# A recurrence and a gated MLP in one kernel: low weight parts and word shifts on VectorE, with a new order of the first part

## The chip, the cores and the metric

The kernel runs on one core of a Trainium2 chip. The metric is the device time of one execution in microseconds. Before the change the median of three runs is 610.35 us (609.67 to 611.15).

## The reference, cut to what matters

A recurrence over 768 tokens (4 batches, 8 heads of 48 channels) gives `y`; its heads, put side by side, are the 3072 x 384 input `x` of a gated MLP with 1536 hidden columns.

```python
for t in range(S):
    cur = einsum('bhd,bhe->bhde', u * k[t], v[t])
    y[t] = einsum('bhd,bhde->bhe', r[t], state + cur)
    state = w * state + einsum('bhd,bhe->bhde', k[t], v[t])
...
gate = 1.0 / (1.0 + np.exp(-(x @ w_gate)))
val = x @ w_val
return gate * val @ w_out
```

All inputs and the output are float32.

## The kernel before, in words

**The recurrence** is computed in chunks of 64 tokens. There are 12 chunks and each is done in two groups of heads, so there are 24 groups, numbered n = 0 to 23. One group takes these steps, each with a letter that the order uses:

- `L.n`, `X.n`: SyncE issues the loads of the chunk by channel (`chan`, three buffers) and by token (`toks`, three buffers).
- `A.n` (ScalarE), `R.n` (`queries`, L265, GpSimd), `k.n` (`keys`, L271, VectorE), `T.n` (`token_keys`, L275, GpSimd): queries and keys times powers of the decay. `A` and `R` write `dec` (two buffers).
- `Z.n` (`scores`): 64 small matmuls into one PSUM tile of two banks, which has one buffer. `K.n` (`keep`, L322, VectorE) copies the masked entries into one of two `score` tiles.
- `I.n` (`apply`) and `O.n` (`outer`): small matmuls into two PSUM banks; with them comes the reading of the old state (`from_state`). `I` gives the chunk's result, `O` what the state gains.
- `h.n` (ScalarE) and `l.n` (`x_low`, L406, VectorE): the result is split into a rounded part and the rest, both written to `xt`, the input of the MLP. `d.n` (ScalarE) and `s.n` (`add_state`, L376, VectorE) decay the state and add to it. `F.n` (`fills`, L417) moves rows of `xt` by DMA on SyncE.

**The MLP** works on tiles of 512 tokens (two chunks), so a tile of tokens needs four groups. Its hidden columns come in 12 weight tiles f of 128. An item i is one token tile with one weight tile. The first token tile takes weight tile 0 in two halves of 256 tokens (items 0 and 1), then weight tiles 1 to 11 whole (items 2 to 12, so item i uses weight tile i - 1). The five other token tiles have 12 items each. One item is

- `U.i` (`up`, L436): 18 matmuls, 9 into each of two PSUM banks (every product is done as three passes over rounded parts and rests),
- `g.i` sigmoid of the first bank (ScalarE, L451), `m.i` product with the second (VectorE, L456), `H.i` the rounded part (ScalarE), `q.i` the rest (`h_low`, L465, GpSimd),
- `D.i` (`down`, L475): 9 matmuls into three accumulator banks.

The banks of `U.i` and of `I.n` come from one ring of three. So the matmuls of a step wait until the readers of the banks three allocations back are through: a sigmoid, a product, or a group's `h`, `l` and `s`.

**The weights** stay in memory once they are prepared, so only the first token tile pays for that. They come as the 64-bit words of double numbers, viewed as pairs of 32-bit words. For weight tile f:

- `W.f` (`load_weights`, L208): the load, 1152 words of 64 bits on each of 128 partitions.
- `c.f` (`scale_words`, L213, ScalarE): the upper word as a float times a power of two, into `wf` (two buffers).
- `j.f` (`join_words`, L219, VectorE): three integer operations on `wf`, on L224, L225 and L226: a shift by 3, the sign, and three bits of the lower word.
- `w.f` (`round_weights`, L228, ScalarE): the rounded part, `whi`. `o.f` (`rest_of_weights`, L234, GpSimd): the rest, `wlo`. Their tile lies in the buffer that the raw words came in.

Weight tile 0 is prepared in halves (`c0`, `j0`, `w0`, `o0`). `w` and `o` work in two halves for all weight tiles.

**The order.** Every engine works through its own instructions in program order, without a scheduler (L86). For the first part, up to item 12, that order is a text, `START` (L41); a loop at L543 calls one step after the other by the table at L525. An engine's own order is `START` with the steps of the others left out. Behind `START` a loop does the other 60 items with the 16 other groups in fixed slots; there `q`, `R` and `T` are on GpSimd.

A branch at the end for unusual decays is not taken with these inputs.

Of the kernel before, what the change touches and what calls it, by code (L numbers as in the profile page):

```python
# [37 lines left out]
HALF, FIRST = 1, 8  # L38
SLOTS = (0, 3, 6, 9)

START = """  # L41
tk tc L.0 L.1 ti.1 X.0 ti.0 A.0 tp X.1 R.0 A.1 W.0 R.1 k.0 tt k.1 tn Z.0 T.0 L.2 T.1 K.0 X.2
c0.0 I.0 c0.1 L.3 j0.0 A.2 R.2 Z.1 h.0 T.2 k.2 w0.0 l.0 O.0 A.3 R.3 K.1 F.0 X.3 o0.0 s.0 Z.2 W.1
j0.1 T.3 I.1 K.2 w0.1 O.1 W.2 h.1 o0.1 k.3 l.1 Z.3 c.1 s.1 F.1 L.4 j.1 I.2 X.4 c.2 W.3 O.2 h.2
R.4 d.2 l.2 T.4 K.3 w.1 F.2 W.4 A.4 o.1 s.2 j.2 I.3 W.5 h.3 O.3 d.3 l.3 w.2 s.3 F.3 L.5 k.4 U.0
c.3 o.2 X.5 j.3 W.6 A.5 Z.4 R.5 g.0 c.4 U.1 T.5 L.6 m.0 w.3 K.4 H.0 o.3 X.6 j.4 g.1 W.7 I.4 O.4
h.4 q.0 d.4 R.6 D.0 m.1 W.8 l.4 H.1 T.6 w.4 s.4 F.4 q.1 k.5 c.5 U.2 o.4 A.6 W.9 j.5 c.6 Z.5 W.10
g.2 D.1 j.6 w.5 U.3 o.5 L.7 m.2 w.6 X.7 K.5 H.2 W.11 o.6 g.3 k.6 c.7 I.5 m.3 H.3 j.7 Z.6 h.5 q.2
d.5 O.5 q.3 D.2 c.8 R.7 A.7 l.5 T.7 s.5 F.5 w.7 K.6 U.4 o.7 j.8 c.9 D.3 g.4 j.9 w.8 I.6 o.8 O.6
h.6 d.6 m.4 w.9 l.6 s.6 F.6 H.4 o.9 c.10 k.7 U.5 j.10 q.4 c.11 Z.7 g.5 m.5 D.4 w.10 K.7 H.5 o.10  # L50
j.11 U.6 q.5 w.11 D.5 g.6 o.11 m.6 I.7 H.6 O.7 h.7 d.7 q.6 l.7 F.7 s.7 U.7 D.6 g.7 m.7 H.7 U.8
q.7 D.7 g.8 m.8 H.8 U.9 q.8 D.8 g.9 m.9 H.9 L.8 X.8 U.10 q.9 D.9 g.10 m.10 H.10 U.11 q.10 D.10
g.11 m.11 H.11 U.12 q.11 A.8 R.8 k.8 T.8 D.11 g.12 m.12 H.12 q.12 D.12
"""


# [1 line left out]
def rwkv_then_moe(ctx: ExitStack, tc: tile.TileContext, wd, ch, tk, wt, rk0, vn0, wd0, out):  # L58
    nc = tc.nc

    const = ctx.enter_context(tc.tile_pool(name="const", bufs=1))
# [31 lines left out]
    w = wu[:, 0]  # L93
# [18 lines left out]
    score = [const.tile([P, 512], F32, name=f"score{i}") for i in range(2)]  # L112

    state = const.tile([P, 4 * N2 * D // 2 + 16], F32, name="state")
    zero = const.tile([P, 1], I32, name="zero")
    table = const.tile([P, 1], F32, name="table")

    def constants():
        make_identity(nc, ident)
        nc.gpsimd.memset(causal, 0.0)  # L120
        nc.gpsimd.affine_select(
            out=causal, in_=causal, compare_op=ALU.is_ge, fill=1.0, base=0,
            pattern=[[-1, P]], channel_multiplier=1,
        )
        for lo in (0, 64):
            nc.gpsimd.tensor_copy(masks[lo : lo + 64, 0], causal[lo : lo + 64, lo : lo + 64])
            nc.gpsimd.tensor_copy(masks[lo : lo + 64, 1], ident[lo : lo + 64, lo : lo + 64])
        nc.gpsimd.memset(zero, 0)
        for t in score:
            nc.gpsimd.memset(t, 0.0)  # L130
        nc.gpsimd.memset(state, 0.0)
        nc.scalar.activation(table, ident[:, 0:1], AF.Sigmoid)
# [7 lines left out]
    tabn = const.tile([P, N2, D], F32, name="tabn")  # L140
# [62 lines left out]

    W3, WH = 3 * DM, 3 * DM // 2
    raw, w32, wparts, whi, wlo = {}, {}, {}, {}, {}
    WHOLE, HALVES = (slice(0, W3),), (slice(0, WH), slice(WH, W3))

    def load_weights(f):  # L208
        raw[f] = wp.tile([P, W3], I64, name="wr", tag=f"w{f or NF - 1}")
        for c in HALVES if f == 0 else WHOLE:  # L210
            nc.sync.dma_start(out=raw[f][:, c], in_=wt[f, :, c])

    def scale_words(f, c):  # L213
        if f not in w32:
            w32[f] = wtmp.tile([P, W3], F32, name="wf")
        words = raw[f].bitcast(F32).rearrange("q (n two) -> q n two", two=2)
        nc.scalar.activation(w32[f][:, c], words[:, c, 1], AF.Copy, scale=2.0**-112)

    def join_words(f, c):  # L219
        words = raw[f].bitcast(I32).rearrange("q (n two) -> q n two", two=2)  # L220
        low, high = words[:, c, 0], words[:, c, 1]
        g = w32[f].bitcast(I32)[:, c]
        none = zero.broadcast_to([P, c.stop - c.start])
        nc.vector.scalar_tensor_tensor(g, g, 3, none, ALU.logical_shift_left, ALU.bitwise_or)  # L224
        nc.vector.scalar_tensor_tensor(g, high, -(2**31), g, ALU.bitwise_and, ALU.bitwise_or)  # L225
        nc.vector.scalar_tensor_tensor(g, low, 29, g, ALU.logical_shift_right, ALU.bitwise_or)  # L226

    def round_weights(f, c):  # L228
        if f not in wparts:
            wparts[f] = wp.tile([P, 2, W3], F32R, name="wx", tag=f"w{f}")  # L230
            whi[f], wlo[f] = wparts[f][:, 0], wparts[f][:, 1]
        nc.scalar.copy(out=whi[f][:, c], in_=w32[f][:, c])  # L232

    def rest_of_weights(f, c):  # L234
        nc.gpsimd.tensor_tensor(wlo[f][:, c], w32[f][:, c], whi[f][:, c], ALU.subtract)  # L235


    xt, dec, ga, yb = {}, {}, {}, {}
# [3 lines left out]
    def bc2(ap):  # L242
        n, m, k = ap.shape
        return ap.unsqueeze(2).broadcast_to([n, m, 2, k])

    def v4(ap):
        return ap.rearrange("q (m t i) -> q m t i", m=4, t=2)

    def dec_of(n):
        if n not in dec:  # L250
            dec[n] = adk.tile([P, 2, 512], F32, name="dec")
        return dec[n]

    def table_of(n):
        return tabk[:, 4 * GROUPS[n][1] : 4 * GROUPS[n][1] + 4]
# [6 lines left out]
                t[:, 1, cs], k[:, cs], AF.Copy, scale=wu[:, 1, 4 * g + m : 4 * g + m + 1]  # L262
            )

    def queries(n):  # L265
        t = dec_of(n)
        nc.gpsimd.tensor_tensor(  # L267
            v4(t[:, 0]), v4(chan[n][:, 0]), bc2(table_of(n)[:, :, ::-1]), ALU.mult
        )

# [1 line left out]
        k = chan[n][:, 1]  # L272
        nc.vector.tensor_tensor(v4(k), v4(k), bc2(table_of(n)), ALU.mult)

    def token_keys(n):  # L275
        k, g = toks[n][:, 0, 0 : 8 * D], GROUPS[n][1]
        nc.gpsimd.tensor_tensor(v4(k), v4(k), bc2(tabn[:, 4 * g : 4 * g + 4]), ALU.mult)  # L277

# [150 lines left out]
    class Moe:  # L431
# [30 lines left out]
            h = self.h[f] = hq.tile([P, 2, 512], F32R, name="h")  # L462
            nc.scalar.copy(out=h[:, 0, c], in_=sg[:, c])  # L463

        def h_low(self, f):  # L465
            c, h = self.cols, self.h[f]
            nc.gpsimd.tensor_tensor(h[:, 1, c], self.sg.pop(f)[:, c], h[:, 0, c], ALU.subtract)  # L467

        def gate(self, f):
            self.sigmoid(f)  # L470
# [18 lines left out]
    def accumulators():  # L489
        return [pacc.tile([P, 512], F32, name=f"acc{d}") for d in range(3)]  # L490
# [12 lines left out]
    items = [(0, h, f) for h, f in halves]  # L503
# [20 lines left out]

    steps = {  # L525
        "L": load_channels, "X": load_tokens, "W": load_weights, "A": bonus_keys, "R": queries,
        "k": keys, "T": token_keys, "Z": scores, "K": keep, "I": apply, "O": outer,
        "d": decay_state, "s": add_state, "h": x_high, "l": x_low, "F": fills, "D": finish,
        "tc": constants, "tk": channel_table, "ti": inverses, "tp": token_powers,
        "tt": token_turn, "tn": token_table,  # L530
        "c": lambda f: [scale_words(f, c) for c in WHOLE],
        "j": lambda f: [join_words(f, c) for c in WHOLE],
        "w": lambda f: [round_weights(f, c) for c in HALVES],
        "o": lambda f: [rest_of_weights(f, c) for c in HALVES],
        "c0": lambda j: scale_words(0, HALVES[j]), "j0": lambda j: join_words(0, HALVES[j]),
        "w0": lambda j: round_weights(0, HALVES[j]), "o0": lambda j: rest_of_weights(0, HALVES[j]),
        "U": lambda i: moe_of(items[i]).up(items[i][2]),
        "g": lambda i: moe_of(items[i]).sigmoid(items[i][2]),
        "m": lambda i: moe_of(items[i]).product(items[i][2]),
# [2 lines left out]
    }  # L542
    for step in START.split():  # L543
        name, _, arg = step.partition(".")
# [52 lines left out]
    with tc.If(bad != 0):  # L597
        with ExitStack() as g:
# [66 lines left out]
            with tc.For_i(0, NC, 2) as c:  # L665
# [11 lines left out]
                m = Moe(x, accumulators(), slice(0, 512))  # L677
# [93 lines left out]
```

## Time and profile before

| | us |
|---|---|
| median of three runs | 610.35 |
| the profiled execution, its own time | 604.38 |
| its span, first to last instruction | 602.4 |
| TensorE matmul busy in the span | 546.7 |
| VectorE busy | 215.6 |
| GpSimd busy | 205.0 |
| ScalarE busy | 191.0 |

In the profile PE is TensorE's matmuls, PEld its weight loads, DVE VectorE, ACT ScalarE, POOL GpSimd and SP SyncE. L with a number is a line of the kernel. A row of the groups gives line, engine, operation, output and inputs, shape and count, then busy time in us and the mean of one in ns, then the engine's idle time just before and what ended it. A row of a timeline gives start and duration in us, then the same names, and in brackets the idle time before it. A row of a stage gives the stretch and its length, then the busy time of each engine with the number of instructions, TensorE's granted clock, the DMA's share and GB/s.

### The profile page before, as it was taken

The page shows a single profiled execution, that of the slowest core. Times are in us where ns is not written, and L with a number is a line of the kernel's source. Part 1 is how long each engine was busy: PE and PEld are TensorE (multiplying, and loading weights), DVE is VectorE, ACT ScalarE, POOL GpSimd, SP SyncE. Part 2 cuts the span into 40 slices and gives each one's busy share as a digit, 9 for nine tenths or more (in the row PEclk, how much of TensorE's full clock was granted, in tenths as well). Part 3 has the DMA queues.
Part 4 walks back from the last instruction along what each step waited for, and adds up shares of the span by engine and source line. Part 5 has one row for each costly group of instructions (what it writes and reads, how often), then busy time and mean ns, then how long its engine had stood idle before and what let it go on. Part 6 is the DMA issues. An engine that isn't in the chain of part 4 may idle for free. (4 is left out here: it accounts for less than half of the span.)

```text
span 602.4 us, 12902 instructions
## 1 busy us (share of the span) xinstructions
PE 546.7 (91%) x5689; PEld 441.6 (73%) x5689; DVE 215.6 (36%) x317; ACT 191.0 (32%) x432; POOL 205.0 (34%) x159
## 2 busy tenths in 40 slices
PE   2747965989979999999999999999999999999994
PEld 2736754778768887878888878888878787888882
DVE  6799799921131232232133133133223112110101
ACT  4364464332232232242233143233233122222211
POOL 6448886732323233133133133133222311121120
PEclk9999768899999999999999999999999999999998
DMA  7479700020060020240020250020250001100001
GB/s 284 181 276 414 317 1 1 10 81 1 5 237 2 1 63 11 81 171 9 1 72 5 78 177 3 1 72 15 67 178 2 1 9 20 50 3 0 1 0 58
DMA packets 13117, 44.55 MB, mean 74 GB/s; under 512 B 2080, under 2 KB 2464, under 8 KB 11648
## 3 DMA queue, kind: packets, MB, share of 16 engines
q1 hardware_dynamic: 13056, 43.66, 20.9%
q8 instruction: 47, 0.77, 0.5%
q14 instruction: 14, 0.11, 0.1%
HBM read 36.58 MB, written 4.72 MB: 69 GB/s over the span
## 5 line engine op out<-in xcount | busy, mean ns | idle before, releaser
L445 PE MATMUL ring<-xt,wx 128*128 128x512 f32 (+1 forms) x1314 | 324.5, 401 | 8.1 <-DVE sg L458 5.6
L445 PEld LDWEIGHTS ring<-xt,wx 128*128 128x128 f32 x1314 | 249.2, 194 | 67.0 <-DVE sg L458 5.7
L467 POOL TENSOR_TENSOR h<-sg,h 128x512 fp32r<-128x512 f32 (+1 forms) x73 | 99.9, 1369 | 345.0 <-ACT h L463 345.0
L483 PE MATMUL acc<-h,wx 128*128 128x512 f32 (+1 forms) x657 | 164.9, 395 | 3.8 <-POOL h L467 3.4
L458 DVE TENSOR_TENSOR sg<-ring,sg 128x512 f32<-128x512 f32 (+1 forms) x73 | 49.9, 683 | 295.9 <-PE ring L445 293.2
L483 PEld LDWEIGHTS acc<-h,wx 128*128 128x128 f32 x657 | 121.7, 190 | 32.3 <-POOL h L467 4.5
L463 ACT CAST h<-sg 128x512 fp32r<-128x512 f32 (+1 forms) x73 | 44.8, 614 | 149.9 <-DVE sg L458 149.9
L454 ACT ACTIVATE sg<-ring 128x512 f32<-128x512 f32 (+1 forms) x73 | 43.2, 591 | 139.7 <-PE ring L445 139.6
L235 POOL TENSOR_TENSOR wx<-wf,wx 128x576 fp32r<-128x576 f32 x24 | 46.8, 1967 | 19.4 <-ACT wx L232 19.3
L325 DVE COPY_PREDICATED score<-masks,sc 128x512 f32<-128x512 int32 x48 | 36.0, 750 | 16.0 <-PE sc L317 15.2
L267 POOL TENSOR_TENSOR dec<-chan,tabk 128x512 f32<-128x512 f32 x24 | 33.6, 1402 | 12.4 <-DMA chan<-in_ch 10.0
L261 ACT ACTIVATE dec<-chan,wu 128x128 f32<-128x128 f32 x96 | 30.8, 401 | 7.7 <-DMA chan<-in_ch 7.3
L408 DVE TENSOR_TENSOR xt<-ring,xt 112x256 fp32r<-112x256 f32 (+1 forms) x52 | 19.9, 417 | 31.2 <-ACT xt L404 31.1
L286 PE MATMUL ring<-dec,state 48*48 48x64 f32 (+1 forms) x704 | 18.4, 235 | 13.7 <-DVE state L381 5.4
L286 PEld LDWEIGHTS ring<-dec,state 48*48 48x48 f32 (+1 forms) x704 | 14.6, 137 | 21.8 <-issue 12.2
L404 ACT CAST xt<-ring 112x256 fp32r<-112x256 f32 (+1 forms) x52 | 17.1, 374 | 41.1 <-PE ring L286 40.9
L225 DVE SCALAR_TENSOR_TENSOR wf<-wr,wf 128x1152 int32<-128x1152 int32 (+1 forms) x13 | 27.2, 2090 | 0.4
L277 POOL TENSOR_TENSOR toks<-toks,tabn 128x384 f32<-128x384 f32 x22 | 23.0, 1048 | 9.3 <-DMA toks<-in_tk 6.2
L371 ACT ACTIVATE state<-state,pw 112x96 f32<-112x96 f32 x80 | 23.4, 366 | 0.0
L286 PEld LDWEIGHTS ring<-score,toks 64*64 64x64 f32 (+1 forms) x768 | 15.2, 143 | 11.0 <-issue 4.9
L232 ACT CAST wx<-wf 128x576 fp32r<-128x576 f32 x24 | 15.0, 671 | 25.5 <-DVE wf L226 25.5
L226 DVE SCALAR_TENSOR_TENSOR wf<-wr,wf 128x1152 int32<-128x1152 int32 (+1 forms) x13 | 22.7, 1750 | 0.4
(45 smaller groups left out, 215.6 us busy)
## 6 DMA issues: line engine op xcount, KB each, us to landing
wr<-in_wt SPq DMA_DIRECT2D x11, 1152.0 KB, 13.3
chan<-in_ch SPq DMA_DIRECT2D x24, 512.0 KB, 4.9
toks<-in_tk SPq DMA_DIRECT2D x24, 400.0 KB, 5.7
out_y<-wf SPq DMA_DIRECT2D x18, 256.0 KB, 2.2
xt<-xt SPq DMA_DIRECT2D x30, 64.0 KB, 2.3
wr<-in_wt SPq DMA_DIRECT2D x2, 576.0 KB, 7.1
xt<-xt SPq DMA_DIRECT2D x12, 32.0 KB, 2.5
wu<-in_wd SPq DMA_DIRECT2D x1, 8.0 KB, 1.9
```

What stands on the lines that cost most here:

```text
L225: nc.vector.scalar_tensor_tensor(g, high, -(2**31), g, ALU.bitwise_and, ALU.bitwise_or)
L235: nc.gpsimd.tensor_tensor(wlo[f][:, c], w32[f][:, c], whi[f][:, c], ALU.subtract)
L261: nc.scalar.activation(t[:, 1, cs], k[:, cs], AF.Copy, scale=wu[:, 1, 4 * g + m : 4 * g + m + 1])
L267: nc.gpsimd.tensor_tensor(v4(t[:, 0]), v4(chan[n][:, 0]), bc2(table_of(n)[:, :, ::-1]), ALU.mult)
L286: nc.tensor.matmul(yb[n][bank][64 * half : 64 * half + m, cs], lhsT, rhs, start=first, stop=stop, skip_group_check=True,)
L325: nc.vector.copy_predicated(t.rearrange("q (b m i) -> q b m i", b=2, m=4), masks[:, m].bitcast(I32).unsqueeze(1).unsqueeze(1).broadcast_to ...
L445: nc.tensor.matmul(o[:, self.cols], w[a][:, g * DM + kt * P : g * DM + (kt + 1) * P], self.x[:, kt, b, self.cols], start=(k == 0), stop=(k ...
L454: nc.scalar.activation(sg[:, c], self.pair[f][0][:, c], AF.Sigmoid)
L458: nc.vector.tensor_tensor(sg[:, c], self.pair.pop(f)[1][:, c], sg[:, c], ALU.mult)
L463: nc.scalar.copy(out=h[:, 0, c], in_=sg[:, c])
L467: nc.gpsimd.tensor_tensor(h[:, 1, c], self.sg.pop(f)[:, c], h[:, 0, c], ALU.subtract)
L483: nc.tensor.matmul(self.acc[d][:, self.cols], w[a][:, 2 * DM + d * P : 2 * DM + (d + 1) * P], h[:, b, self.cols], start=(f == 0 and k == 0 ...
```

## The change

Four things change.

1. The rest of a weight tile (`rest_of_weights`) can be computed on VectorE. `START` calls that form, `ov`, for weight tiles 1, 2, 3, 4, 5, 7, 8, 10 and 11; both halves of tile 0 and tiles 6 and 9 stay on GpSimd.
2. The shift of the words is a `tensor_scalar` and no longer a `scalar_tensor_tensor` that ORs a broadcast zero; the zero tile is gone.
3. `w` and `o` of weight tiles 1 to 11 work on whole tiles, not halves.
4. `START` is a new order. It also calls VectorE forms of three other steps: queries of groups 0, 1 and 3 (`Rv`), token keys of groups 3 to 7 (`Tv`), rests of h of items 0, 1, 4, 5 and 12 (`qv`). U.0 now stands ahead of the scores of group 3, and U.1, U.2 and U.3 ahead of the second part of group 4.

The loop behind `START` is as before. The diff, cut to its core (the names in the table of steps that only lose their list of slices are left out):

```diff
 START = """
+tc L.0 L.1 X.0 X.1 W.0 tk L.2 X.2 A.0 ti.1 Rv.0 A.1 k.0 ti.0 Z.0 Rv.1 k.1 tp L.3 c0.1 c0.0 K.0 tt
+tn T.0 j0.1 I.0 T.1 Z.1 h.0 A.2 R.2 O.0 l.0 w0.1 K.1 T.2 F.0 X.3 W.1 o0.1 W.2 s.0 W.3 L.4 j0.0 I.1
+O.1 h.1 k.2 X.4 s.1 w0.0 Z.2 l.1 A.3 o0.0 L.5 K.2 c.1 F.1 U.0 k.3 Rv.3 c.2 Tv.3 Z.3 j.1 g.0 I.2
+m.0 w.1 K.3 O.2 R.4 H.0 X.5 h.2 qv.0 W.4 ov.1 d.2 W.5 L.6 l.2 c.3 s.2 F.2 j.2 I.3 A.4 O.3 R.5 h.3
+X.6 d.3 W.6 l.3 W.7 W.8 w.2 s.3 F.3 j.3 U.1 A.5 D.0 g.1 U.2 m.1 w.3 ov.2 H.1 ov.3 c.4 qv.1 c.5 k.4
+Tv.4 Z.4 g.2 k.5 Tv.5 D.1 L.7 m.2 K.4 H.2 U.3 q.2 j.4 Z.5 g.3 m.3 w.4 I.4 K.5 H.3 O.4 h.4 R.6 ov.4
+D.2 X.7 d.4 W.9 W.10 q.3 W.11 A.6 l.4 s.4 F.4 c.6 j.5 I.5 O.5 h.5 R.7 d.5 A.7 l.5 s.5 F.5 w.5 k.6
+U.4 Tv.6 j.6 Z.6 g.4 ov.5 w.6 D.3 m.4 c.7 o.6 K.6 H.4 U.5 j.7 c.8 g.5 qv.4 w.7 j.8 I.6 O.6 h.6 D.4
+d.6 m.5 w.8 l.6 s.6 F.6 H.5 ov.7 U.6 qv.5 c.9 ov.8 k.7 c.10 Tv.7 j.9 Z.7 g.6 D.5 m.6 U.7 w.9 K.7
+H.6 o.9 j.10 g.7 q.6 c.11 I.7 O.7 h.7 D.6 d.7 m.7 l.7 H.7 s.7 F.7 w.10 q.7 j.11 U.8 ov.10 D.7 w.11
+g.8 ov.11 U.9 m.8 H.8 q.8 D.8 g.9 m.9 H.9 L.8 X.8 U.10 q.9 D.9 g.10 m.10 H.10 U.11 q.10 D.10 g.11
+m.11 H.11 U.12 q.11 A.8 R.8 k.8 T.8 D.11 g.12 m.12 H.12 qv.12 D.12
 """
...
-    zero = const.tile([P, 1], I32, name="zero")
...
-        nc.gpsimd.memset(zero, 0)
...
-        none = zero.broadcast_to([P, c.stop - c.start])
-        nc.vector.scalar_tensor_tensor(g, g, 3, none, ALU.logical_shift_left, ALU.bitwise_or)
+        nc.vector.tensor_scalar(g, g, 3, None, ALU.logical_shift_left)
...
-    def rest_of_weights(f, c):
-        nc.gpsimd.tensor_tensor(wlo[f][:, c], w32[f][:, c], whi[f][:, c], ALU.subtract)
+    def rest_of_weights(f, c, eng=nc.gpsimd):
+        eng.tensor_tensor(wlo[f][:, c], w32[f][:, c], whi[f][:, c], ALU.subtract)
...
-        "w": lambda f: [round_weights(f, c) for c in HALVES],
-        "o": lambda f: [rest_of_weights(f, c) for c in HALVES],
+        "w": lambda f: round_weights(f, ALL), "w0": lambda j: round_weights(0, HALVES[j]),
+        "o": lambda f: rest_of_weights(f, ALL), "o0": lambda j: rest_of_weights(0, HALVES[j]),
+        "ov": lambda f: rest_of_weights(f, ALL, nc.vector),
+        "Rv": lambda n: queries(n, nc.vector), "Tv": lambda n: token_keys(n, nc.vector),
+        "qv": lambda i: moe_of(items[i]).h_low(items[i][2], nc.vector),
```

`queries`, `token_keys` and `h_low` take the engine as an argument in the same way as `rest_of_weights`, with GpSimd as the default.

More of the change, by code (lines that the diff above doesn't have):

```diff
@@ L41 @@
 START = """
[L42 to L53, printed above, removed]
+tc L.0 L.1 X.0 X.1 W.0 tk L.2 X.2 A.0 ti.1 Rv.0 A.1 k.0 ti.0 Z.0 Rv.1 k.1 tp L.3 c0.1 c0.0 K.0 tt
[10 more added lines that the diff above has]
+m.11 H.11 U.12 q.11 A.8 R.8 k.8 T.8 D.11 g.12 m.12 H.12 qv.12 D.12
 """
@@ L205, in rwkv_then_moe @@
     raw, w32, wparts, whi, wlo = {}, {}, {}, {}, {}
-    WHOLE, HALVES = (slice(0, W3),), (slice(0, WH), slice(WH, W3))
+    ALL, HALVES = slice(0, W3), (slice(0, WH), slice(WH, W3))
     def load_weights(f):
         raw[f] = wp.tile([P, W3], I64, name="wr", tag=f"w{f or NF - 1}")
-        for c in HALVES if f == 0 else WHOLE:
+        for c in HALVES if f == 0 else (ALL,):
             nc.sync.dma_start(out=raw[f][:, c], in_=wt[f, :, c])
@@ L263, in bonus_keys, with queries @@
             )
-    def queries(n):
+    def queries(n, eng=nc.gpsimd):
         t = dec_of(n)
-        nc.gpsimd.tensor_tensor(
+        eng.tensor_tensor(
             v4(t[:, 0]), v4(chan[n][:, 0]), bc2(table_of(n)[:, :, ::-1]), ALU.mult
@@ L273, in keys, with token_keys @@
         nc.vector.tensor_tensor(v4(k), v4(k), bc2(table_of(n)), ALU.mult)
-    def token_keys(n):
+    def token_keys(n, eng=nc.gpsimd):
         k, g = toks[n][:, 0, 0 : 8 * D], GROUPS[n][1]
-        nc.gpsimd.tensor_tensor(v4(k), v4(k), bc2(tabn[:, 4 * g : 4 * g + 4]), ALU.mult)
+        eng.tensor_tensor(v4(k), v4(k), bc2(tabn[:, 4 * g : 4 * g + 4]), ALU.mult)
     begun = set()
@@ L463, in h_high, with h_low @@
             nc.scalar.copy(out=h[:, 0, c], in_=sg[:, c])
-        def h_low(self, f):
+        def h_low(self, f, eng=nc.gpsimd):
             c, h = self.cols, self.h[f]
-            nc.gpsimd.tensor_tensor(h[:, 1, c], self.sg.pop(f)[:, c], h[:, 0, c], ALU.subtract)
+            eng.tensor_tensor(h[:, 1, c], self.sg.pop(f)[:, c], h[:, 0, c], ALU.subtract)
         def gate(self, f):
@@ L530, in rwkv_then_moe @@
         "tt": token_turn, "tn": token_table,
-        "c": lambda f: [scale_words(f, c) for c in WHOLE],
-        "j": lambda f: [join_words(f, c) for c in WHOLE],
-        "w": lambda f: [round_weights(f, c) for c in HALVES],
-        "o": lambda f: [rest_of_weights(f, c) for c in HALVES],
-        "c0": lambda j: scale_words(0, HALVES[j]), "j0": lambda j: join_words(0, HALVES[j]),
-        "w0": lambda j: round_weights(0, HALVES[j]), "o0": lambda j: rest_of_weights(0, HALVES[j]),
+        "c": lambda f: scale_words(f, ALL), "c0": lambda j: scale_words(0, HALVES[j]),
+        "j": lambda f: join_words(f, ALL), "j0": lambda j: join_words(0, HALVES[j]),
+        "w": lambda f: round_weights(f, ALL), "w0": lambda j: round_weights(0, HALVES[j]),
+        "o": lambda f: rest_of_weights(f, ALL), "o0": lambda j: rest_of_weights(0, HALVES[j]),
+        "ov": lambda f: rest_of_weights(f, ALL, nc.vector),
+        "o0v": lambda j: rest_of_weights(0, HALVES[j], nc.vector),
+        "Rv": lambda n: queries(n, nc.vector), "Tv": lambda n: token_keys(n, nc.vector),
+        "qv": lambda i: moe_of(items[i]).h_low(items[i][2], nc.vector),
         "U": lambda i: moe_of(items[i]).up(items[i][2]),
```

## The prediction

> **What bounds the kernel now.** I read the page first: totals, then the span in 40 slices.
>
> ```profile
> span 602.4 us, 12902 instructions
> PE 546.7 (91%) x5689; PEld 441.6 (73%) x5689; DVE 215.6 (36%) x317; ACT 191.0 (32%) x432; POOL 205.0 (34%) x159
> PE   2747965989979999999999999999999999999994
> DVE  6799799921131232232133133133223112110101
> PEclk9999768899999999999999999999999999999998
> ```
>
> Over the span TensorE is the bound, but its holes lie in the first eight slices of 15 us, and there VectorE is at 7 to 9 tenths. So I asked the stages: busy time of each engine in three stretches.
>
> ```profile
> 0.00:126.90 126.90, 107.97 (x121) 0.91 0.46 176
> 125.00:160.00 35.00, 35.00 (x153) 28.32 (x152) 5.54 (x10) 9.38 (x21) 9.81 (x8) 1.00 0.12 35
> 160.00:602.00 442.00, 428.66 (x4138) 343.88 (x4136) 103.47 (x190) 122.28 (x287) 110.06 (x89) 0.99 0.15 47
> ```
>
> The first row is VectorE alone: 108.0 of 126.9 us busy. The others begin with TensorE: full, and the changed order ends before 165 us. So only the moment counts at which TensorE gets its full row of weight tiles. TensorE in order of time:
>
> ```profile
> 42.99 2.29 PE L445 MATMUL ring<-xt,wx 128*128 128x256 f32 x9
> 104.05 6.44 PE L445 MATMUL ring<-xt,wx 128*128 128x512 f32 x18 [5.59 <-DVE sg L458]
> 124.66 4.45 PE L445 MATMUL ring<-xt,wx 128*128 128x512 f32 x18
> 131.00 4.36 PE L445 MATMUL ring<-xt,wx 128*128 128x512 f32 x18
> 155.99 4.36 PE L445 MATMUL ring<-xt,wx 128*128 128x512 f32 x18
> ```
>
> These rows are steps U.0 (its first half), U.5, U.7, U.8 and U.12. From U.8 to U.12 they follow each other at (155.99 - 131.00) / 4 = 6.25 us, with TensorE full. Both orders are the same for TensorE from U.8 on, so **the gain is the shift of U.8's start**, 131.0 now.
>
> Why 131.0? U.5's 5.59 us of waiting is for a product on VectorE, which stands in line behind the weight words. VectorE and GpSimd in order of time:
>
> ```profile
> 30.59 1.36 DVE L224 SCALAR_TENSOR_TENSOR wf<-wf,zero 128x1152 int32<-128x1152 int32 x1 [3.35 <-ACT wf L217]
> 31.98 1.36 DVE L225 SCALAR_TENSOR_TENSOR wf<-wr,wf 128x1152 int32<-128x1152 int32 x1
> 40.05 2.44 DVE L225 SCALAR_TENSOR_TENSOR wf<-wr,wf 128x1152 int32<-128x1152 int32 x1
> 43.80 1.72 DVE L408 TENSOR_TENSOR xt<-ring,xt 48x256 fp32r<-48x256 f32 x4
> 72.20 1.36 DVE L224 SCALAR_TENSOR_TENSOR wf<-wf,zero 128x1152 int32<-128x1152 int32 x1 [2.58 <-ACT wf L217]
> 126.28 0.62 DVE L381 TENSOR_TENSOR state<-state,ring 112x192 f32<-112x192 f32 x2 [0.32 <-ACT state L371]
> ```
>
> ```profile
> 27.64 1.40 POOL L235 TENSOR_TENSOR wx<-wf,wx 128x576 fp32r<-128x576 f32 x1
> 37.40 3.88 POOL L235 TENSOR_TENSOR wx<-wf,wx 128x576 fp32r<-128x576 f32 x2
> ```
>
> A word operation takes 1.36 us at 31.98, when GpSimd stands still (its row at 27.64 ends at 29.04), and 2.44 at 40.05, during GpSimd's 3.88 us. GpSimd pays too: 3.88 for two pieces that take 1.40 alone. What that costs in all is in the groups by line and shape:
>
> ```profile
> L224 DVE SCALAR_TENSOR_TENSOR wf<-wf,zero 128x1152 int32<-128x1152 int32 x11 | 17.8, 1619 | 7.1 <-ACT wf L217 7.0
> L225 DVE SCALAR_TENSOR_TENSOR wf<-wr,wf 128x1152 int32<-128x1152 int32 x11 | 25.0, 2270 | 0.4
> L226 DVE SCALAR_TENSOR_TENSOR wf<-wr,wf 128x1152 int32<-128x1152 int32 x11 | 21.2, 1930 | 0.4
> L235 POOL TENSOR_TENSOR wx<-wf,wx 128x576 fp32r<-128x576 f32 x24 | 46.8, 1967 | 19.4 <-ACT wx L232 19.3
> L267 POOL TENSOR_TENSOR dec<-chan,tabk 128x512 f32<-128x512 f32 x24 | 33.6, 1402 | 12.4 <-DMA chan<-in_ch 10.0 <-PE sc L317 1.4 <-DVE tabk L160 1.1
> L277 POOL TENSOR_TENSOR toks<-toks,tabn 128x384 f32<-128x384 f32 x22 | 23.0, 1048 | 9.3 <-DMA toks<-in_tk 6.2 <-ACT tabn L182 3.1
> L467 POOL TENSOR_TENSOR h<-sg,h 128x512 fp32r<-128x512 f32 x71 | 96.2, 1355 | 345.0 <-ACT h L463 345.0
> L273 DVE TENSOR_TENSOR chan<-chan,tabk 128x512 f32<-128x512 f32 x24 | 17.3, 726 | 4.7 <-ACT dec L261 4.4
> L458 DVE TENSOR_TENSOR sg<-ring,sg 128x512 f32<-128x512 f32 x71 | 49.0, 691 | 295.1 <-PE ring L445 293.2 <-ACT sg L454 1.9
> ```
>
> The three word operations take 17.8 + 25.0 + 21.2 = 64.0 us, where 33 x 1.36 = 44.9 would do: 19.1 us of VectorE go to meeting GpSimd.
>
> **The change part by part**, on VectorE up to step s.7, whose end (126.9) gives group 7's second PSUM bank back. In the new order that bank is what the second half of U.8 needs (it was U.7's). The old time is the start, and I add what differs.
>
> The shift. It loses its second tensor. No wide scalar operation is in the trace; the nearest rows are the 1.36 above and a copy with one source in SBUF:
>
> ```profile
> 8.58 0.42 DVE L169 COPY sg<-pw 64x512 f32<-64x512 f32 x1
> ```
>
> That is 512 elements in 0.42 us, where two-tensor L273 takes 0.726 for 512 at its mean. Operations with two tensors go from 0.691 (L458, 512) to 1.36 (1152): 1.05 ns an element and 0.15 us fixed. The copy less that 0.15 is 0.53 ns an element, so 1152 come to 0.76. Bounds 0.76 and 1.36; I take 0.76, since it too has one source and both ends in SBUF. Ten whole tiles precede s.7 and two halves: 10 x -0.6 and 2 x -0.3 = -6.6.
>
> [...]
>
> The low part. Seven of the nine moved ones stand ahead of s.7 (tiles 1, 2, 3, 4, 5, 7, 8): two tensors of 1152, as the word operations, 7 x 1.36 = +9.5. Four stay on GpSimd (both halves of tile 0, tiles 6 and 9).
>
> Other moved steps: three queries, of L273's shape, 3 x 0.73 = 2.2; five token keys, 384 instead of 512 elements, 5 x 0.55 = 2.8; of h's low parts two whole (0.69, like L458) and two halves (0.42, estimated by the same 1.05 ns and 0.15 us), 2.2. Together +7.2.
>
> The order: tile 11's words now follow s.7 (-3 x 1.36 = -4.1) and product 7 precedes it (+0.7). Sum of the work: -6.6 + 9.5 + 7.2 - 4.1 + 0.7 = +6.7.
>
> Meetings with GpSimd. Up to s.7 it did 24 low halves, 8 queries, 8 token keys and 7 h: 24 x 1.97 + 8 x 1.40 + 8 x 1.05 + 7 x 1.36 = 76 us. It keeps six halves' worth, 5 queries, 3 token keys and 3 h: 11.8 + 7.0 + 3.1 + 4.1 = 26. By that 19.1 becomes 6.5; VectorE has more operations that can be met, so I take 8 (bounds 0 and 26): -11.
>
> VectorE's waits: 126.9 - 108.0 = 18.9 now. The 3.35 us at 30.59 end with words scaled after a late load; four small steps (keep 2, keys 3, queries 3, token keys 3) now stand ahead of them. The 2.58 at 72.20 go back to the low part on GpSimd, whose queue is gone. New ones: product 0 stands ahead of everything from group 3's scores on, and its sigmoid stands behind the scaling of tile 2, which waits for the load:
>
> ```profile
> 29.32 1.24 ACT L217 ACTIVATE wf<-wr 128x1152 f32<-128x1152 f32 x1 [3.72 <-DMA wr<-in_wt]
> 33.76 1.27 ACT L217 ACTIVATE wf<-wr 128x1152 f32<-128x1152 f32 x1 [3.20 <-DMA wr<-in_wt]
> 18.70 4.41 SPq L412 DMA_DIRECT2D xt<-xt x6
> ```
>
> The loads of tiles 1 and 2 stand behind group 0's six fills on SyncE, before and after; these come somewhat sooner, as two word halves no longer both precede x_low 0. So tile 2 is scaled by about 33 and VectorE loses 1 to 2 us. Products 2 and 3 wait for U.2 and U.3, 2 to 3 more. With the start and 3 to 4 for hand-overs I take 11: -8.
>
> ```profile
> 2.70 0.17 DVE L151 TENSOR_SCALAR pw<-wu 128x8 f32<-128x8 f32 x1 [1.81 <-DMA wu<-in_wd]
> ```
>
> This first operation starts at 2.70, in both orders. Loads 9 to 11 now stand behind group 7's, whose buffers come free with step O.4 (behind U.1, D.0, U.2 and U.3, so about 70). Tile 9's words stand two tiles of words (7 us) and a few small steps ahead of 114.6, so past 100: nothing waits. Uncovered, VectorE would wait for the load.
>
> **Sum:** +6.7 - 11 - 8 = -12.3, so s.7 ends at 114.6 and U.8 starts there: 16.4 us earlier than 131.0. Can TensorE be there? The tile's second half of x was ready at 43.80 + 1.72 = 45.5; behind it stand U.1 (2 x 2.29, as slow as U.0), D.0 (9 of the same, 2.3), six weight tiles at 6.25 and four groups of five blocks like this one, 3.3 each:
>
> ```profile
> 170.18 0.65 PE L317 MATMUL sc<-chan,dec 48*64 48x64 f32 x32
> ```
>
> That is 58 us, or 103.5. So 11 us are in hand and VectorE decides. Behind s.7 VectorE still has tile 11's words and two low parts, 6.2 us, under U.8, D.7 and U.9, and U.12 is the first to need the last. GpSimd's dropped memset (0.1) is hidden. The halves of tiles 1 to 11 become whole for ScalarE and GpSimd: a fixed cost less each, hidden.
>
> The profiled execution took 604.38 us, its span 602.4 and 2.0 around it; the median is 6.0 above it. 604.4 - 16.4 = 588.0 for such an execution, 610.35 - 16.4 = **594** for the median.
>
> **Rivals.**
>
> *VectorE loses all that GpSimd works.* At 40.05 an operation of 1.36 lost 1.08, nearly GpSimd's piece of 1.40. If every piece still there blocks it whole, 26 instead of 8: U.8 comes 18 later, at 132.6, less the 8 us of new waits that such delays would fill: 124.6, gain 6.4, 604. For it: nine low parts and nine smaller two-tensor steps leave VectorE without a two-tensor operation for little of the time; against: today 76 us of GpSimd cost 19. [...]
>
> *The shift gains nothing,* 1.36 as before: +6.6, so 600.5. Inside the range.
>
> *Slower: VectorE takes over GpSimd's wait for the high part.*
>
> ```profile
> POOL wx L235 <- ACT wx L232: 19.3, 8, 3.5
> ACT wf L217 <- POOL wx L235: 11.6, 3, 5.8
> ```
>
> The low part needs ScalarE's rounding, which stands in ScalarE's line behind sigmoids and casts that wait for TensorE. GpSimd waited 19.3 us for it in 8 waits, 2.4 each, harmlessly. On VectorE the product, the masks' copy and the state stand behind such a wait, and TensorE's banks behind those. Nine times 2.4 is 21.7, against 16.4: 5 us slower, 615. It decides from 1.8 us each. For: the second wait above, scaling held up by low parts, is a ring that now goes through VectorE. Against: in the new order one to six VectorE steps stand between a tile's words and its low part, mostly longer than the rounding's 1.25.
>
> *The order brings nothing* (U.8 at 131 for other waits of the same size): 610.
>
> **How the numbers follow.** Forecast 0.60, shift without gain 0.12, meetings in full 0.11, VectorE waits 0.11, nothing 0.06. About 0.2%, 1.2 us, can be told from no change. Faster: 0.83 (the first three); same 0.06; slower 0.11. The range starts at 586 (no meetings at all, 8 us less) and reaches to 606, past the two smaller gains; about 0.18 is left out.
>
> **What would show it.** Right: the shift near 0.76; L225 and L226 near 1.36 to 1.7 in the mean; VectorE's low parts without waits of ScalarE before them; U.8 at 112 to 118 and 6.25 per tile behind it; GpSimd about 30 us busy in the first 115. Wrong: idle time of VectorE ahead of low parts that adds up to over 10 us; L225 still above 2.2; TensorE's granted clock low through 50 to 110, so that six tiles at about 10 us use up the 11 in hand; or a hole behind U.8.

## The result, and the profile after

The changed kernel takes 586.25 us in the median of four runs (585.33 to 588.98). The kernel before takes 610.01 (608.68 to 611.15). The ratio is 0.9619, 95% interval 0.958 to 0.9657: 23.8 us less by the medians. The profiled execution of the changed kernel took 585.8 us with a span of 584.0.

The page of the changed kernel, the totals and the slices (each 14.6 us now):

```profile
span 584.0 us, 12860 instructions
PE 539.5 (92%) x5689; PEld 435.8 (75%) x5689; DVE 212.5 (36%) x339; ACT 190.0 (33%) x421; POOL 147.2 (25%) x125
PE   3755988999899999999999999999999999999994
DVE  7787999932313313312312313312313212101101
PEclk9966998999799999999999999999999999999998
```

TensorE is dense from the fifth slice on, where before it had holes up to the seventh. VectorE is as full as it was, GpSimd lost 58 us. TensorE in order of time shows U.7, U.8 and U.12, and behind them U.13 and U.14, the item behind group 8's first scores.

```profile
102.68 4.36 PE L443 MATMUL ring<-xt,wx 128*128 128x512 f32 x18
111.31 4.45 PE L443 MATMUL ring<-xt,wx 128*128 128x512 f32 x18
136.44 4.36 PE L443 MATMUL ring<-xt,wx 128*128 128x512 f32 x18
144.75 4.36 PE L443 MATMUL ring<-xt,wx 128*128 128x512 f32 x18
...
155.13 6.22 PE L443 MATMUL ring<-xt,wx 128*128 128x512 f32 x18
```

U.8 starts at 111.31 instead of 131.00, 19.7 us earlier, and (136.44 - 111.31) / 4 = 6.28 us per weight tile follow, as before. The groups by line and shape:

```profile
L223 DVE SCALAR_TENSOR_TENSOR wf<-wr,wf 128x1152 int32<-128x1152 int32 x11 | 17.0, 1547 | 0.4
L224 DVE SCALAR_TENSOR_TENSOR wf<-wr,wf 128x1152 int32<-128x1152 int32 x11 | 15.9, 1444 | 0.4
L233 DVE TENSOR_TENSOR wx<-wf,wx 128x1152 fp32r<-128x1152 f32 x9 | 12.4, 1385 | 0.0
L222 DVE TENSOR_SCALAR wf<-wf 128x1152 int32<-128x1152 int32 x11 | 11.9, 1082 | 3.3 <-ACT wf L216 3.3
L233 POOL TENSOR_TENSOR wx<-wf,wx 128x1152 fp32r<-128x1152 f32 x2 | 5.4, 2694 | 27.9 <-ACT wx L230 27.9
```

The sign step fell from 2270 to 1547 ns in the mean, the lower bits from 1930 to 1444; alone they take 1.36. The low parts on VectorE take 1385 and wait for nothing. VectorE's own timeline shows the shift alone and the shift met by GpSimd, and the one wait that the prediction did not have:

```profile
31.11 0.76 DVE L222 TENSOR_SCALAR wf<-wf 128x1152 int32<-128x1152 int32 x1 [3.31 <-ACT wf L216]
53.94 0.42 DVE L456 TENSOR_TENSOR sg<-ring,sg 128x256 f32<-128x256 f32 x1 [3.96 <-PE ring L443]
104.24 2.67 DVE L222 TENSOR_SCALAR wf<-wf 128x1152 int32<-128x1152 int32 x1
111.84 0.61 DVE L379 TENSOR_TENSOR state<-state,ring 112x192 f32<-112x192 f32 x2
```

The last row is step s.7, which ends at 112.45; the stage up to there, VectorE alone:

```profile
0.00:112.45 112.45, 98.07 (x139) 0.89 0.54 199
```

### The profile page after: what moved, and what is told of

Its sections match the earlier page's. It is cut to its first block, busy times and chain, and to the rows that moved or that the text cites. A ratio compares the mean times of both kernels' runs of the same rounds, so it can differ in the third digit from the quotient of the medians.

```text
span 584.0 us, 12860 instructions
## 1 busy us (share of the span) xinstructions
PE 539.5 (92%) x5689; PEld 435.8 (75%) x5689; DVE 212.5 (36%) x339; ACT 190.0 (33%) x421; POOL 147.2 (25%) x125
## 5 line engine op out<-in xcount | busy, mean ns | idle before, releaser
L465 POOL TENSOR_TENSOR h<-sg,h 128x512 fp32r<-128x512 f32 x68 | 89.6, 1318 | 363.9 <-ACT h L461 363.9
L481 PE MATMUL acc<-h,wx 128*128 128x512 f32 (+1 forms) x657 | 163.0, 392 | 0.4 <-POOLq L597 0.4
L461 ACT CAST h<-sg 128x512 fp32r<-128x512 f32 (+1 forms) x73 | 44.8, 614 | 146.5 <-DVE sg L456 146.5
L265 POOL TENSOR_TENSOR dec<-chan,tabk 128x512 f32<-128x512 f32 x21 | 29.1, 1385 | 20.6 <-DMA chan<-in_ch 12.7
L402 ACT CAST xt<-ring 112x256 fp32r<-112x256 f32 (+1 forms) x52 | 17.2, 375 | 45.5 <-PE ring L284 45.4
L315 PE MATMUL sc<-dec,chan 48*64 48x64 f32 x768 | 17.4, 232 | 8.5 <-DVE chan L271 7.2
L284 PEld LDWEIGHTS ring<-score,toks 64*48 64x48 f32 (+1 forms) x768 | 15.4, 143 | 12.3 <-issue 6.9
L284 PE MATMUL ring<-score,toks 64*48 64x64 f32 (+1 forms) x768 | 18.8, 242 | 5.4 <-DVE score L323 4.0
L315 PEld LDWEIGHTS sc<-dec,chan 48*64 48x64 f32 x768 | 14.9, 146 | 10.3 <-DVE chan L271 7.2
L275 POOL TENSOR_TENSOR toks<-toks,tabn 128x384 f32<-128x384 f32 x17 | 18.0, 1060 | 9.6 <-ACT tabn L181 8.7
L216 ACT ACTIVATE wf<-wr 128x1152 f32<-128x1152 f32 (+1 forms) x13 | 15.3, 1192 | 15.3 <-DMA wr<-in_wt 10.7
```

Source lines behind the costliest of these rows:

```text
L265: eng.tensor_tensor(v4(t[:, 0]), v4(chan[n][:, 0]), bc2(table_of(n)[:, :, ::-1]), ALU.mult)
L284: nc.tensor.matmul(yb[n][bank][64 * half : 64 * half + m, cs], lhsT, rhs, start=first, stop=stop, skip_group_check=True,)
L315: nc.tensor.matmul(sc[64 * gm : 64 * gm + 64, be, o : o + C], kk[row, cs : cs + C], rr[row, cs : cs + C], start=True, stop=True,)
L465: eng.tensor_tensor(h[:, 1, c], self.sg.pop(f)[:, c], h[:, 0, c], ALU.subtract)
L481: nc.tensor.matmul(self.acc[d][:, self.cols], w[a][:, 2 * DM + d * P : 2 * DM + (d + 1) * P], h[:, b, self.cols], start=(f == 0 and k == 0 ...
```

## The experiments

Theory A is that of the prediction: VectorE's work, its meetings with GpSimd and its waits set when TensorE gets going. Theory B: the order did it and the engines are incidental. Theory C came up with the second set: what stays on GpSimd blocks VectorE for its whole length. Each kernel was timed beside the kernel before on the same chip; as the kernel before moved a little from set to set, kernels of different sets are compared by their ratios to it. By the intervals of the ratios, a difference between two kernels of different sets is good to about 3 us.

**The parts alone.** Two parts have no run of their own: the small steps on VectorE in the old order, and whole tiles in place of halves. The diffs leave out lines that only bring the zero tile back or take it away, and the `eng` argument. First the order (with whole tiles): the changed kernel with the old engines and the old shift:

```diff
-        "ov": lambda f: rest_of_weights(f, ALL, nc.vector),
-        "Rv": lambda n: queries(n, nc.vector), "Tv": lambda n: token_keys(n, nc.vector),
-        "qv": lambda i: moe_of(items[i]).h_low(items[i][2], nc.vector),
+        "ov": lambda f: rest_of_weights(f, ALL),
+        "Rv": lambda n: queries(n), "Tv": lambda n: token_keys(n),
+        "qv": lambda i: moe_of(items[i]).h_low(items[i][2]),
...
-        nc.vector.tensor_scalar(g, g, 3, None, ALU.logical_shift_left)
+        none = zero.broadcast_to([P, c.stop - c.start])
+        nc.vector.scalar_tensor_tensor(g, g, 3, none, ALU.logical_shift_left, ALU.bitwise_or)
```

> The new order alone: every operation on its old engine (low parts, queries, token keys and rests of h on GpSimd) and the shift with its zero tile. Theory A (VectorE's work and its meetings with GpSimd set the time; the order only interleaves): GpSimd's 76 us of work are back, so the three word operations are at 1.6 to 2.2 us in the mean again, and a good part of the gain of 23.8 us is gone: 594 to 602 us. Theory B (the order does nearly all): within 3 us of the changed kernel, 586 to 589 us.

Measured: 600.6 us, ratio 0.9867 (0.983 to 0.9905), about 8 us less than before and inside theory A's range. Theory B falls: the order alone brings a third of the gain.

The shift alone, on the kernel before:

```diff
-        nc.vector.scalar_tensor_tensor(g, g, 3, none, ALU.logical_shift_left, ALU.bitwise_or)
+        nc.vector.tensor_scalar(g, g, 3, None, ALU.logical_shift_left)
```

> The kernel before with the shift as a scalar operation and nothing else. Theory A: 0.6 us less in each of 11 whole tiles and 0.3 in two halves, 7 us of a VectorE that is busy 108 of the first 127 us; half of it or more comes through: 603 to 607 us. Theory B: no change, 609 to 611 us, since product and masks stand in the same places behind other work.

Measured: 600.52 us, ratio 0.9863 (0.9825 to 0.99). One operation in 13 places (11 whole tiles, two halves) is worth as much as the whole new order. The 8.3 us are a little more than theory A gave it (3 to 7 us).

The low parts alone, in the old order of the kernel before:

```diff
-        "o": lambda f: [rest_of_weights(f, c) for c in HALVES],
+        "o": lambda f: [rest_of_weights(f, c, nc.gpsimd if f in (6, 9) else nc.vector) for c in HALVES],
```

> The kernel before, old order, with the low parts of weight tiles 1, 2, 3, 4, 5, 7, 8, 10 and 11 on VectorE (in halves, as before) at the same places of the order. Theory A: +13 us of VectorE's own work against some 10 us fewer of meetings: 605 to 613 us. The rival of a wait that moves to VectorE: each low part waits 1.8 to 2.4 us for ScalarE's rounding, since the old order leaves no steps between: 620 to 630 us.

Measured: 604.07 us, ratio 0.9926 (0.9897 to 0.9955), 4.5 us less, a little better than theory A's range. The rival of the prediction, a wait for ScalarE that moves to VectorE, is out: in this kernel's VectorE timeline one pair of low parts out of nine has such a wait at all, and in the changed kernel none.

```profile
117.46 1.43 DVE L235 TENSOR_TENSOR wx<-wf,wx 128x576 fp32r<-128x576 f32 x2 [0.80 <-ACT wx L232]
```

**The parts taken away** from the changed kernel. With the old shift:

```diff
-        nc.vector.tensor_scalar(g, g, 3, None, ALU.logical_shift_left)
+        none = zero.broadcast_to([P, c.stop - c.start])
+        nc.vector.scalar_tensor_tensor(g, g, 3, none, ALU.logical_shift_left, ALU.bitwise_or)
```

> The changed kernel with the old shift and its zero tile; low parts, small steps and order as changed. The shift alone was worth 7.9 us on the kernel before. Theory A (VectorE decides in both kernels): 10 shifts of 0.6 us ahead of the last state step, and more to be met by GpSimd: 5 to 9 us above the changed kernel's 586.2, 591 to 595. Rival (with the new order VectorE has slack, TensorE decides): under 3 us, 586 to 589.

Measured: 590.34 us, ratio 0.9696 (0.9671 to 0.9721). Against 0.9619 that is about 4.7 us, just under the 5 to 9 us of theory A, and the intervals alone do not quite shut out the rival's 3. The trace shows that VectorE still decides: U.8, which waits for nothing in the changed kernel, waits here for product 7 on VectorE.

```profile
114.62 6.00 PE L446 MATMUL ring<-xt,wx 128*128 128x512 f32 x18 [2.14 <-DVE sg L459]
```

The changed kernel with its low parts on GpSimd:

```diff
-        "ov": lambda f: rest_of_weights(f, ALL, nc.vector),
+        "ov": lambda f: rest_of_weights(f, ALL),
```

> The changed kernel with all low parts on GpSimd, at the same places of the order. Theory A: VectorE's own work falls by 7 x 1.36 = 9.5 us up to the last state step, its meetings grow by 7 x 2.7 us of GpSimd's work (at 0.26 to 0.5 us each, 5 to 10), and the scaling of a tile two further on waits for GpSimd: 586 to 592 us. Theory C (a low part on GpSimd blocks VectorE for its whole 2.7 us, and so moving it is what pays): 592 to 598.

Measured: 592.64 us, ratio 0.9753 (0.9728 to 0.9778), about 8 us above the changed kernel. That is theory C's range. The groups of VectorE up to 130 us and ScalarE's waits in that stretch:

```profile
L223 DVE SCALAR_TENSOR_TENSOR wf<-wr,wf 128x1152 int32<-128x1152 int32 x11 | 24.8, 2255 | 0.4
L224 DVE SCALAR_TENSOR_TENSOR wf<-wr,wf 128x1152 int32<-128x1152 int32 x11 | 21.5, 1955 | 0.4
L222 DVE TENSOR_SCALAR wf<-wf 128x1152 int32<-128x1152 int32 x11 | 12.8, 1162 | 2.0 <-ACT wf L216 2.0
```

```profile
ACT wf L216 <- POOL wx L233: 7.1, 4, 3.6
```

The word operations are back at 2.26 and 1.96 us (2.27 and 1.93 in the kernel before). They cost 59.1 us instead of 44.8: 14.3 more for nine pieces, so 1.6 us of VectorE for each piece that GpSimd does, against 1.36 if VectorE does it. Other rows grew too: the four rests of h on VectorE took 6.5 us instead of 2.2. In all, VectorE is busy 105.3 us up to s.7 (which ends at 116.94 here), 7.2 more than in the changed kernel, although seven low parts of 9.7 us in all are gone from it. That is 16.9 us for seven pieces, 2.4 for each. And ScalarE waits 7.1 us for GpSimd before it can scale the next words, 1.7 in the changed kernel. So moving a low part saves VectorE about 1 us and takes GpSimd out of that chain.

The changed kernel with its small steps on GpSimd:

```diff
-        "Rv": lambda n: queries(n, nc.vector), "Tv": lambda n: token_keys(n, nc.vector),
-        "qv": lambda i: moe_of(items[i]).h_low(items[i][2], nc.vector),
+        "Rv": lambda n: queries(n), "Tv": lambda n: token_keys(n),
+        "qv": lambda i: moe_of(items[i]).h_low(items[i][2]),
```

> The changed kernel with the queries, token keys and rests of h back on GpSimd, low parts and shift as changed. Theory A: 7.2 us less work on VectorE against some 12 us more of GpSimd's, of which a third to a half comes back as meetings; token keys 3 to 7 and queries 0 and 1 come later on GpSimd: 584 to 589 us. Theory C (each piece on GpSimd blocks VectorE whole): 590 to 594.

Measured: 590.14 us, ratio 0.9708 (0.9684 to 0.9733), about 5 us above the changed kernel: inside theory C's range, at its lower edge. Up to 130 us the words, the low parts and the keys take VectorE 71.0 us instead of 62.7: 8.3 more, against 7.1 that the steps themselves cost on VectorE.

The changed kernel with the last two low parts on VectorE too:

```diff
-U.4 Tv.6 j.6 Z.6 g.4 ov.5 w.6 D.3 m.4 c.7 o.6 K.6 H.4 U.5 j.7 c.8 g.5 qv.4 w.7 j.8 I.6 O.6 h.6 D.4
+U.4 Tv.6 j.6 Z.6 g.4 ov.5 w.6 D.3 m.4 c.7 ov.6 K.6 H.4 U.5 j.7 c.8 g.5 qv.4 w.7 j.8 I.6 O.6 h.6 D.4
...
-H.6 o.9 j.10 g.7 q.6 c.11 I.7 O.7 h.7 D.6 d.7 m.7 l.7 H.7 s.7 F.7 w.10 q.7 j.11 U.8 ov.10 D.7 w.11
+H.6 ov.9 j.10 g.7 q.6 c.11 I.7 O.7 h.7 D.6 d.7 m.7 l.7 H.7 s.7 F.7 w.10 q.7 j.11 U.8 ov.10 D.7 w.11
```

> The changed kernel with the low parts of weight tiles 6 and 9 on VectorE as well, at the same places. In the changed kernel these two pieces of 2.7 us on GpSimd stand beside a shift of 1.42 (0.76 alone) and beside a shift of 2.67 and a sign step of 2.31 (1.36 alone): 3.5 us of VectorE lost for two operations that would cost 2.7. Theory A (a piece on GpSimd costs VectorE about what is lost beside it): no difference that counts, 584.5 to 587. Theory C (a piece blocks VectorE whole and the order around it): 582 to 584. Rival (VectorE is full, so any work on it costs): 588 to 590.

Measured: 586.19 us, ratio 0.9643 (0.9612 to 0.9673), the same as the changed kernel and inside theory A's range. The two meetings with these pieces are gone (the shift that took 2.67 takes 0.75 at the same place), and the low parts themselves stand there instead. One of them meets a rest of h on GpSimd (104.24 to 105.53) and takes 2.47 us, not 1.36:

```profile
104.28 2.47 DVE L233 TENSOR_TENSOR wx<-wf,wx 128x1152 fp32r<-128x1152 f32 x1
106.67 0.75 DVE L222 TENSOR_SCALAR wf<-wf 128x1152 int32<-128x1152 int32 x1
```

The sign step of 2.31 us, which the expectation put down to the low part, had met that same rest of h, which came later there (106.25 to 108.05). Without such a meeting it takes 1.36.

**The wait that was not predicted.** Product 1 waits 3.96 us because U.1 starts only at 50.04. U.1 needs the second half of x, and so group 2's fills. TensorE in the changed kernel, and the landing of the fills between 20 and 60 us:

```profile
50.04 3.79 PE L443 MATMUL ring<-xt,wx 128*128 128x256 f32 x18 [7.16 <-DVE wf L224]
```

```profile
DMA to landing us min/median/max: 2.5/8.3/10.0
```

The row names the words of tile 3, which end at the same moment (49.99); before, the fills of this stretch landed in 2.0/2.5/3.7 us. So there were two readings, told apart by moving the loads in the changed kernel's order:

```diff
-m.0 w.1 K.3 O.2 R.4 H.0 X.5 h.2 qv.0 W.4 ov.1 d.2 W.5 L.6 l.2 c.3 s.2 F.2 j.2 I.3 A.4 O.3 R.5 h.3
+m.0 w.1 K.3 O.2 R.4 H.0 X.5 h.2 qv.0 ov.1 d.2 L.6 l.2 c.3 s.2 F.2 W.4 W.5 j.2 I.3 A.4 O.3 R.5 h.3
```

> The changed kernel with the loads of weight tiles 4 and 5 issued behind the six fills of group 2 and not ahead of them. In the changed kernel U.1 starts at 50.0, 4.1 us after x_low 3, and the fills' landing took up to 10.0 us. If the fills lie behind 2.3 MB of weights (theory A): their landing is back at 2 to 4 us, U.1 starts at about 46.5, product 1 waits under 1 us and the time is 2 to 4 us less than the changed kernel's, 582 to 584. If U.1 waits for the words of tile 3 (rival; they end at 50.0 too): no change of U.1, 586 us.

Measured: 581.24 us, ratio 0.9541 (0.9502 to 0.9579). The landing is back at 2.0/2.8/4.2 us, U.1 runs from 44 on, and product 1 waits for nothing:

```profile
44.04 3.78 PE L443 MATMUL ring<-xt,wx 128*128 128x256 f32 x16 [0.62 <-DVE xt L406]
```

```profile
48.01 0.41 DVE L456 TENSOR_TENSOR sg<-ring,sg 128x256 f32<-128x256 f32 x1
```

The gain is a little more than theory A's 2 to 4 us. The releaser in the row was the wrong one; it was the DMA. In the three kernels above that have the shift, the low parts or the small steps taken away, the loads stand as in the changed kernel, and there the row of U.1 does name the fills, with waits of 7.97 to 8.25 us. Two loads of 1.15 MB ahead of six fills of 32 KB cost 4.7 us.

**The hole behind U.13**, which is in both kernels: TensorE waits for the masks' copy of group 8 (1.63 us before, 1.64 in the changed kernel). D.12 can stand there. The edit is made to the kernel with the fills first.

```diff
-m.11 H.11 U.12 q.11 A.8 R.8 k.8 T.8 D.11 g.12 m.12 H.12 qv.12 D.12
+m.11 H.11 U.12 q.11 A.8 R.8 k.8 T.8 D.11 g.12 m.12 H.12 qv.12
...
-        if i > n0:
-            finish(i - 1)
+        finish(i - 1)
```

> The kernel with the fills first (581.2 us), and D.12 behind the scores of group 8 in the loop, not ahead of U.13. In the changed kernel TensorE waits 1.64 us for the masks' copy of group 8 there, then 0.72, and behind that its next 18 matmuls took 6.22 instead of 4.36 us. Theory A (the hole is what lets the clock fall): D.12 fills it, 2 to 4 us less, 577 to 579.5. Rival (the matmuls only move, the wait stands elsewhere): 581.

Measured: 575.66 us, ratio 0.9462 (0.944 to 0.9484); against 0.9541 that is about 5 us less than with the fills first, more than theory A's 2 to 4. TensorE's timeline there first without, then with it:

```profile
147.12 0.68 PE L284 MATMUL ring<-score,toks 64*64 64x64 f32 x32 [1.63 <-DVE score L323]
...
150.11 6.84 PE L443 MATMUL ring<-xt,wx 128*128 128x512 f32 x18
```

```profile
143.36 2.32 PE L481 MATMUL acc<-h,wx 128*128 128x512 f32 x9
145.61 0.68 PE L284 MATMUL ring<-score,toks 64*64 64x64 f32 x32
...
146.67 2.36 PE L443 MATMUL ring<-xt,wx 128*128 128x512 f32 x9
149.58 2.33 PE L443 MATMUL ring<-xt,wx 128*128 128x512 f32 x9 [0.55 <-DVE state L379]
```

The 1.63 us are gone, and the 18 matmuls behind them take 4.69 us instead of 6.84, close to the 4.36 of the others. The granted clock is 1.00 from 115 to 150 us; at the same hole of the changed kernel it was 0.69 (152 to 163 us). This version is the fastest of all, 5.4% under the kernel before.

**The profile that the prediction started from.** Its execution took 604.38 us, the other runs 605 to 612. So the unchanged kernel was profiled again:

> The kernel before, unchanged, for a second profile of it. Its first profiled execution took 604.4 us, its other runs 606 to 611 and 608.4 in the median. In that profile the 18 matmuls behind group 8's first scores took 4.46 us; in eight profiles of seven other orders and of the changed kernel they took 6.2 to 7.2 wherever the same hole stands ahead of them. Theory A (the first profile is of an execution that kept its clock there): this profile shows 6 to 7 us at that place, and the span is 2 to 5 us longer, 605 to 608. Rival (the profile itself shortens the execution): 4.4 us and 602.4 again.

Measured: 606.78 us in the median, ratio 0.9982 (0.9958 to 1.0007), span 606.7. U.8 and the item behind the hole in this second profile:

```profile
125.51 5.56 PE L445 MATMUL ring<-xt,wx 128*128 128x512 f32 x18
130.91 2.25 PE L483 MATMUL acc<-h,wx 128*128 128x512 f32 x9
133.00 4.35 PE L445 MATMUL ring<-xt,wx 128*128 128x512 f32 x18
...
177.43 6.77 PE L445 MATMUL ring<-xt,wx 128*128 128x512 f32 x18
```

U.8 stands at 133.00 and not at 131.00, and the item behind the hole takes 6.77 and not 4.46: 2.0 + 2.3 of the 4.3 us by which the spans differ. In the first profile the granted clock was 1.00 around U.7 (121 to 135 us) and around the item behind the hole (172 to 182). In the second it was 0.89 in the mean from 160 to 180, where the first has 1.00, and U.7's matmuls took 5.56 us instead of 4.45. So the first profile was of an execution that kept its clock behind the hole and ran through U.7 at full pace. Not all of the 2.0 is in U.7's matmuls: 0.4 of it was there ahead of group 7's, behind a longer wait for GpSimd (0.88 us instead of 0.21).

## Why the prediction was right, point by point

**The path** was right in its main line and wrong in its last step. U.8's start carries the gain, and 6.28 us per tile follow. VectorE's s.7 ended at 112.45 against 114.6 forecast. But s.7 did not hold U.8 in the changed kernel:

```profile
93.49 6.01 PE L443 MATMUL ring<-xt,wx 128*128 128x512 f32 x18 [1.97 <-DVE sg L456]
108.95 2.33 PE L481 MATMUL acc<-h,wx 128*128 128x512 f32 x9
```

U.8 started at 111.31, as soon as the 9 matmuls at 108.95 had ended, and ran through in 4.45 us. Its second half, which alone needs s.7, began at about 113.5 (an estimate, half of 4.45 behind the start), one microsecond after s.7. "11 us are in hand" failed: TensorE was forecast ready at 103.5 and came at 111.3. U.1 started at 50.04 instead of 45.5, and the way from there to U.8 took 61.3 us instead of 58, with waits for VectorE that the sum did not have: 1.57 us for a state step ahead of U.4's second half and 1.97 for product 5 ahead of U.6, whose matmuls then took 6.01 us instead of 4.36. So VectorE held TensorE at these earlier steps, and TensorE held VectorE at product 1. Both came to U.8 within about 1 us of each other. That s.7 ended so near U.8's start was in part luck; that VectorE's time counts is shown by the parts taken away.

**The terms.** The shift took 0.76 alone (the row at 31.11), as forecast. The seven low parts took 9.7 us (9.5 forecast), the small steps 2.1 + 2.8 + 2.2 = 7.1 (7.2). The meetings: ten shifts 2.7, ten of each other word operation 2.1 and 0.9 over their time alone, seven low parts 0.2: 5.9 us, 8 forecast. VectorE was busy 98.1 us, not the 103.7 of the sum: 2.1 from the meetings, 1.5 from the table of powers (0.8 us instead of 2.3 for its two products of 256), which GpSimd no longer meets at the start, and the rest from keys that are met less (0.69 us instead of 0.79 in the mean of eight) and from rows that overlap by up to 0.1 us where one follows at once.

**The waits** were 112.45 - 98.07 = 14.4 us, 11 forecast. The step that failed there is "behind group 0's six fills on SyncE, before and after", with nothing on group 2's: I followed the loads of tiles 4 and 5 as something that is early enough, not as something that others stand behind on the DMA engines. That is the 3.96 us before product 1.

**The size.** Forecast 16.4, measured 23.8. The measured 586.25 lies at the range's lower end, 586, which stood for no meetings at all. There were 5.9 us of meetings, so it is luck that this bound was wide enough. In the two profiles U.8 moved by 19.7, 3.3 more than forecast: s.7 ended 2.2 earlier (5.6 less work, 3.4 more waits), and U.8 started 1.1 ahead of its end. The rest, 4.1, was in making the sum on one profiled execution and taking it off the median. That execution was 4.3 us shorter than a second one of the same kernel, mostly for the matmuls behind the hole (4.46 us instead of 6.77) and of U.7 (4.45 instead of 5.56), and the changed kernel's profile had no such luck at the same hole (6.22 us, granted clock 0.69 from 152 to 163). Of the signs that the prediction named, U.8 at 111.3 lies just ahead of its 112 to 118, and GpSimd was busy 30.5 us in the first 115, as forecast. Against the second profile U.8 moved 21.7 and the span 22.7.

**The rivals.** "The shift gains nothing" and "VectorE takes over GpSimd's wait" are out by their rows. "VectorE loses all that GpSimd works" was wrong as a total (5.9 of the 26 us), but right in each place looked at: the shift of 2.67 us started at 104.24 beside GpSimd's low part,

```profile
103.61 2.68 POOL L233 TENSOR_TENSOR wx<-wf,wx 128x1152 fp32r<-128x1152 f32 x1 [18.24 <-ACT wx L230]
```

which ended at 106.29, and the shift ended at 106.91, 0.62 behind it, as if it had waited for the whole piece. The shifts at 61.69, 84.57 and 112.36 also end 0.61 to 0.62 behind the GpSimd piece that had begun ahead of them, and the two-tensor word operations at 41.93 and 106.95 end 1.22 and 1.21 behind theirs. In the total it was less, since pieces also fell beside steps that show no loss: the queries at 36.91 beside x_low 2, the rest of h at 60.71 beside keep 4. What each part was worth could not be read from the parts' own durations: alone, the order, the shift and the low parts gave 8.1, 8.3 and 4.5 us; taken away, the shift, the low parts and the small steps cost 4.7, 8.2 and 5.4.

## What to carry to other kernels

When two engines slow each other, price an operation on the lesser engine by what it takes from the fuller one beside it (here 1.6 us of VectorE in the word operations alone, 2.4 in all, for each low part on GpSimd), and compare that with the price of doing it there (1.36). When one engine is said to have time in hand, put its own waits for the other engine into its sum; here the forecast's 11 us were gone. When loads are moved forward, list what stands behind them on the DMA engines: here six transfers of 32 KB behind two of 1.15 MB cost 4.7 us, and the wait was shown under another name. Before a sum is made against one profiled execution, look how its time stands to the other runs; here it was 6 us below the median, and that was the larger part of the miss (4.1 of 7.4 us).

## What the runs showed of the hardware

Behind a hole of 1.63 us and a second one of 0.7 to 1.8, with 1 to 2 us of small matmuls between them, TensorE's next 18 matmuls took 6.0 to 7.2 us instead of 4.36 in ten profiles out of eleven that have it; in one they took 4.46. The granted clock around them was 0.69 in the changed kernel (152 to 163 us). Filling the first hole was worth about 5 us, three times the hole. The two profiles of the kernel before, at the same place, show both: 4.46 us with a granted clock of 1.00 in the mean from 160 to 180 us, and 6.77 us with 0.89. No run shows what decides between them.
